# The rows of maxima are sent from SyncE's queue, with another pace for the key and value work

## The chip, the cores and the metric

The kernel runs on one core of one Trainium2 chip. The core has five engines that run at the same time, each through its own list of instructions in order: TensorE (PE, with its weight loads shown apart as PEld), VectorE (DVE), ScalarE (ACT), GpSimd (POOL) and SyncE (SP). SP does no arithmetic here: it issues transfers (DMAs). An instruction that needs another engine's result, or a transfer's, waits for a semaphore, and everything behind it on its engine waits too. The metric is the time of one execution on the device in microseconds (us), lower is better.

## The reference, cut to what matters

Two attention blocks over the same 2048 tokens of width 1024, each with 32 heads of width 32, mixed by a gate per token. Block A is linear attention, block B softmax attention:

```
qkv = x @ wqkv                       # both blocks, own weights
A:  kv  = einsum("bhsd,bhse->bhde", phi(k), v);  z = sum over s of phi(k)
    o   = (phi(q) @ kv) / (phi(q) . z + 1e-6)
B:  p   = softmax(q @ k.T * 32**-0.5);  o = p @ v
g   = sigmoid((x * gate_w).sum(-1))
out = g * (oA @ A_wo) + (1 - g) * (oB @ B_wo)
```

All of it is in float32. The kernel splits an operand into a high and a low part of a narrower type and makes three products of them (L158 to L160: high with high, high with low, low with high).

## The kernel before

**Stages.** First come the projections of block B (L437 to L439 and L475 to L477, up to about 490 us), whose queries and keys go to DRAM (`qk`) and come back head by head. Then the 32 heads of block B run, one after the other. Beside them, in the gaps of PE, runs the linear work of block A ("linear matmuls" below: L993, L158, L159, L160): first the keys and values (`kv`), then the queries (`q`), then the output product (`o`). The end is the output product of block B with the gate.

**A head of block B.** The scores are made twice. `maxima()` makes them with queries in the partitions (L1214), and DVE reduces each 128x512 tile to its row maximum (L1224): 64 tiles a head. `heads_()` makes them again with keys in the partitions (L1403), 64 tiles; ACT takes the exponential of each (L1407), four products a tile of keys give the weighted values (L1508), GpSimd adds the exponentials up (L1452, L1456), with a share done by DVE (L1468). The stream of maxima is 12 or more tiles ahead: while head h is in its second scores, the maxima of head h + 1 are made.

**The rows of maxima.** A maximum is subtracted inside the second scores' matmul: the operand `q` of head h (a tile `big`, three of them in turn) has 96 rows of queries, and rows 96 and 97 hold the negative maxima, as a high and a low part. `rows()` puts them there. DVE reduces the four partial maxima (L1229); PE transposes them (L1235) into a bank; ACT writes the high part `mh` (L1237); DVE makes the low part `ml` (L1240); then two transfers of 8 KB write the two rows (L1246). `mh` and `ml` are two parts of one tile, `m_both`. The first L1403 of the head waits for both transfers.

**What sets the order.** The order on each engine is made when the program is built, by a planner that runs the streams (`maxima`, `heads_`, `linear`, `output`) against clocks of its own (`T`, one for each engine, `use()` adds a cost). A stream yields the time at which it could go on; the planner takes one that can go on now and lags most. Work for DVE is put into a list (`defer`) and taken when DVE is free by the clocks; `tasks` are small jobs that run when their time has come on PE's clock. `rows_ready[h]` is the time at which the planner thinks that the rows have landed: the first second-score of head h isn't taken before it. In the kernel before, the sending is such a task, `send`, which adds 1.1 to ACT's clock.

**The pace of the linear work.** `goal` grows with each tile of second scores by `rates[...]`: 1.4 linear matmuls a tile for `kv` (RATE_KV), 2.6 for `q`, and for `o` what is left (L1674).

**Other lines that are named below.** L833 copies one key/value output out of its bank, and L663 to L665 and L841 follow it; L946 writes a partial sum back into a bank. In the query work DVE divides (L1136, L1137) after ACT has added 1e-6 to the denominators (L1128), PE transposes the result (L797), ACT and DVE split it (L799, L802), and it goes to DRAM as `oA` (L804). L1517 copies the finished values of a head out of their bank. L754 and L759 fold the keys and values into the output weight. L1304 to L1313 turn the sums of a head, L1319 (GpSimd) scales the head's values and L1321 (SP) stores them. L1171 and L1173 load the queries of a later head, L1185 its keys, L658 the operands of `q` and `o` units (two transfers of 512 KB a unit), L1150 stores a result of `o`, and L737 loads output weights.

Of the kernel before, what the change touches and what calls it, by code (L numbers as in the profile page):

```python
# [18 lines left out]
P = 128  # L19
DH = 32  # L20
# [8 lines left out]
WO_SLOT = 4  # L29
RESERVE = 56.0  # L30
RATE_Q = 2.6
RATE_KV = 1.4
AHEAD = {"head": 0, "max": 6, "lin": 40, "kvout": 0, "out": 0}
MM = 0.2275
AV, AV_SWITCH = 0.865, 0.35
# [13 lines left out]
def kernel(  # L49
# [19 lines left out]
    nc = tc.nc  # L69
# [12 lines left out]
    def f32(ap):  # L82
        return ap.bitcast(F32)
# [42 lines left out]
    mh, ml = m_both[:NT], m_both[DH:]  # L126
# [41 lines left out]
    def use(eng, cost, *after):  # L168

        if eng == "dve":  # L170
            after_own[0], own_now[0] = own_now[0], False
        T[eng] = max(T[eng], *after, 0.0) + cost
        return T[eng] + LATENCY[eng]
# [9 lines left out]
    def defer(fn, at, cost=0.6, rank=1, prev=None):  # L183
        item = Later(fn, at, cost, rank, prev)
        later.append(item)
        return item
# [42 lines left out]
    def bank_at(seed=False):  # L229

        times = [ended(readers[b], free[b]) for b in RING if not held[b] and (whole[b] or not seed)]
        return min((at for at in times if at is not None), default=None)

    def take(seed=False, part=False, kept=False):

        idle = [b for b in RING if not held[b] and (whole[b] or not seed)]
        times = {b: ended(readers[b], free[b]) for b in idle}
        b = min(idle, key=lambda b: (times[b] is None, times[b] or 0.0))
        need(readers[b])
        free[b] = ended(readers[b], free[b])  # L240
        readers[b].clear()
        held[b] = True
        whole[b] = whole[b] if kept else not part
        return b

    def give(b, at=0.0, items=()):

        held[b] = False
        free[b] = max(free[b], at)
        readers[b].extend(items)  # L250

    def both(*times):

        return None if None in times else max(times)
# [207 lines left out]
    for np_, js in enumerate(PAIRS):  # L462
# [3 lines left out]
        for pos, k in enumerate(KORDER):  # L466
            while v_at[0] == pos:
                v_next(next(steps))
            i, half = divmod(pos, 2)
# [690 lines left out]
    rows_ready = [None] * H  # L1160
    s_done, st_done = [0], [0]
    tasks = []
# [64 lines left out]
    def rows(h, q, m):  # L1227
        end = use("dve", 0.14)
        nc.vector.tensor_reduce(m, mx[h % 2], AX.X, ALU.max, negate=True)  # L1229

        def turn():
            b = take(part=True)
            pm = bank[b]
            end = use("pe", 0.12, free[b])
            nc.tensor.transpose(pm[:NT, :P], m, ident)  # L1235
            end = use("act", 0.2, end)
            nc.scalar.copy(mh, pm[:NT, :P])  # L1237

            def low(end):
                nc.vector.tensor_sub(ml, pm[:NT, :P], f32(mh))  # L1240

                def send():
                    rows_ready[h] = use("act", 1.1, end) + 2.5
                    for i, part in enumerate((mh, ml)):
                        r = 3 * DH + i
                        nc.scalar.dma_start(f32(q[r:r + 1, :]).rearrange("o (t c) -> o t c", c=P), f32(part))  # L1246

                tasks.append((lambda: end + 0.2, send))

            give(b, 0.0, [defer(low, end, 0.2, 0)])  # L1250

        tasks.append((lambda: both(bank_at(), end), turn))
# [419 lines left out]
    rates = {"q": RATE_Q, "v": 0.0}  # L1672
    rates["kv"] = RATE_KV
    rates["o"] = (cost["o"] - RESERVE) / (steps - cost["q"] / RATE_Q - cost["kv"] / RATE_KV)  # L1674
    goal = [warm]
# [110 lines left out]
```

## Time and profile before

| | us |
|---|---|
| median of 3 runs | 2856.14 (2854.89 to 2862.61) |
| profiled execution, its own time | 2858.8 |
| profiled execution, span | 2857.0 |

| engine | busy us | share of the span |
|---|---|---|
| PE (matmul) | 2820.2 | 99% |
| DVE | 2277.9 | 80% |
| POOL | 1962.8 | 69% |
| ACT | 1691.0 | 59% |

The transfers have a share of 53.6% on SP's queue (q1 in the profile, 394608 packets) and 0.1% on ACT's (q10, 2048 packets: the rows of maxima alone). The granted clock of PE is 0.996 over the run.

A row of the timeline has the start and length in us, the engine, the line, what is done, the tile written and those read; in brackets the idle time ahead of it on its engine and who ended it. A row of the waits has who waited, for whom, the total in us, how many times and the longest. A row of the stretches has the length and for each engine the busy time with the number of instructions, then PE's clock, the DMA share and GB/s. "SPq" and "ACTq" are instructions that issue transfers.

### The profile page before, as it was taken

To read this page: it belongs to the slowest core of one execution; us is meant where nothing else is said; L and a number is where in the kernel's file an instruction comes from. 1 tells how busy PE (TensorE), PEld (TensorE's weight loads), DVE (VectorE), ACT (ScalarE), POOL (GpSimd) and SP (SyncE) were. 2 spreads that over 40 slices of the span, in tenths; PEclk is the share of its full clock that TensorE was granted. 3 is DMA by queue.
4 is the path that set the end of the run, shared out by engine and by line. 5 is a ranking of instruction groups with operands and counts; after the bars stand their busy time and mean duration, and the time that the engine had idled before them with its cause. 6 is when DMAs were issued, how large, how long until landed. Compare 5 with 4: busy or idle time off the path is not lost. (4 is left out here: it accounts for less than half of the span.)

```text
span 2857.0 us, 45633 instructions
## 1 busy us (share of the span) xinstructions
PE 2820.2 (99%) x15552; PEld 2004.8 (70%) x15552; DVE 2277.9 (80%) x3972; ACT 1691.0 (59%) x3206; POOL 1962.8 (69%) x733
## 2 busy tenths in 40 slices
PE   9999999999999999999999999999999999999999
PEld 8888887766666666667666676676666666666687
DVE  7667646888888888888887787788999999997743
ACT  5334320766777677766777566666666666666421
POOL 1212222689999999998989677777889898986000
PEclk9999999999999999999999999999999999999999
DMA  6987888555565433554533456446543434423663
GB/s 194 293 263 230 279 260 274 149 156 155 175 181 162 134 112 105 177 147 132 158 109 114 147 179 205 144 142 180 160 131 111 119 108 143 107 94 122 216 213 103
DMA packets 396890, 470.14 MB, mean 165 GB/s; under 512 B 109366, under 2 KB 240950, under 8 KB 393526
## 3 DMA queue, kind: packets, MB, share of 16 engines
q1 hardware_dynamic: 394608, 466.69, 53.6%
q8 instruction: 123, 2.02, 0.3%
q14 instruction: 111, 0.91, 0.1%
q10 hardware_dynamic: 2048, 0.53, 0.1%
HBM read 318.77 MB, written 146.79 MB: 163 GB/s over the span
## 5 line engine op out<-in xcount | busy, mean ns | idle before, releaser
L1456 POOL TENSOR_TENSOR big<-big,big 128x1536 f32<-128x1536 f32 (+1 forms) x434 | 1557.8, 3589 | 134.7 <-ACT big L1407 113.5
L1224 DVE TENSOR_REDUCE mx<-bank 128x1 f32<-128x512 f32 x2048 | 1344.9, 687 | 246.9 <-PE bank L1214 237.0
L1407 ACT ACTIVATE big<-bank 128x512 f32<-128x512 f32 x2048 | 1163.0, 604 | 437.6 <-PE bank L1403 363.5
L1403 PE MATMUL bank<-big,big 128*128 128x512 f32 x2048 | 807.2, 400 | 6.6 <-ACT big L1407 4.5
L1214 PE MATMUL bank<-big,big 128*128 128x512 f32 x2048 | 802.9, 394 | 9.6 <-DVE mx L1224 6.1
L1403 PEld LDWEIGHTS bank<-big,big 128*128 128x128 f32 x2048 | 382.5, 188 | 171.9 <-issue 44.2
L1214 PEld LDWEIGHTS bank<-big,big 128*128 128x128 f32 x2048 | 385.5, 188 | 107.9 <-DVE mx L1224 19.9
L1508 PE MATMUL bank<-big,mid 128*32 128x512 f32 x4096 | 459.9, 594 | 0.0
L993 PE MATMUL bank<-big,big 128*128 128x512 f32 x1344 | 452.4, 391 | 0.1
L158 PE MATMUL bank<-big,big 128*128 128x512 f32 x896 | 353.1, 394 | 5.7 <-ACT big L270 3.6
L160 PE MATMUL bank<-big,big 128*128 128x512 f32 x896 | 352.1, 393 | 0.5 <-DMA big<-xs 0.5
L1468 DVE TENSOR_TENSOR bank<-bank,big 128x256 f32<-128x256 f32 (+1 forms) x697 | 326.8, 469 | 32.1 <-ACT big L1407 1.0
L159 PE MATMUL bank<-big,big 128*128 128x512 f32 x896 | 351.9, 393 | 0.0
L1508 PEld LDWEIGHTS bank<-big,mid 128*32 128x32 f32 x4096 | 131.8, 110 | 271.6 <-issue 271.3
L993 PEld LDWEIGHTS bank<-big,big 128*128 128x128 f32 x1344 | 251.0, 188 | 54.2 <-ACT bank L946 1.4
L271 DVE TENSOR_TENSOR big<-mid,big 128x512 fp32r<-128x512 f32 x216 | 153.3, 732 | 82.5 <-ACT big L270 82.4
L1452 POOL TENSOR_TENSOR big<-big,big 128x1536 f32<-128x1536 f32 (+1 forms) x31 | 111.6, 3599 | 146.4 <-ACT big L1407 146.4
L416 POOL TENSOR_TENSOR mid<-mid,mid 128x512 f32<-128x512 f32 x16 | 20.7, 1292 | 278.2 <-DVE big L271 251.7
L158 PEld LDWEIGHTS bank<-big,big 128*128 128x128 f32 x896 | 169.5, 189 | 44.9 <-ACT big L270 4.0
L160 PEld LDWEIGHTS bank<-big,big 128*128 128x128 f32 x896 | 169.4, 189 | 36.2 <-DMA big<-xs 1.9
L159 PEld LDWEIGHTS bank<-big,big 128*128 128x128 f32 x896 | 169.7, 189 | 35.6 <-issue 0.8
L270 ACT CAST big<-mid 128x512 fp32r<-128x512 f32 x216 | 130.3, 624 | 94.2 <-POOL mid L417 54.5
(112 smaller groups left out, 2451.4 us busy)
## 6 DMA issues: line engine op xcount, KB each, us to landing
big<-xs SPq DMA_DIRECT2D x80, 512.0 KB
qk<-mid SPq DMA_DIRECT2D x128, 256.0 KB
big<-xt SPq DMA_DIRECT2D x128, 256.0 KB
big<-oA SPq DMA_DIRECT2D x64, 512.0 KB
big<-qk SPq DMA_DIRECT2D x96, 256.0 KB
big<-qk SPq DMA_DIRECT2D x384, 64.0 KB
big<-xs SPq DMA_DIRECT2D x96, 256.0 KB
mid<-in_b_wqkv SPq DMA_DIRECT2D x88, 256.0 KB
```

What stands on the lines that cost most here:

```text
L158: yield nc.tensor.matmul(ps, sh, mh_, start=(kt == 0), stop=False)
L159: yield nc.tensor.matmul(ps, sh, ml_, start=False, stop=False)
L160: yield nc.tensor.matmul(ps, sl, mh_, start=False, stop=(kt == NK - 1))
L271: eng.tensor_sub(lo, src, f32(hi))
L993: nc.tensor.matmul(bank[b], x_, w, start=(k == 0 and j == 0 and not seeded), stop=(k == HK - 1 and j == 2), skip_group_check=seeded)
L1214: nc.tensor.matmul(bank[b], q[:, t * P:(t + 1) * P], k[:, j * C:(j + 1) * C], start=True, stop=True)
L1224: nc.vector.tensor_reduce(m[:, t, j:j + 1], bank[b], AX.X, ALU.max)
L1403: nc.tensor.matmul(bank[b], k[:, t * P:(t + 1) * P], q[:, j * C:(j + 1) * C], start=True, stop=True)
L1407: nc.scalar.activation(pr_t[i][:, j * C:(j + 1) * C], bank[b], AF.Exp, scale=SCALE)
L1456: nc.gpsimd.tensor_add(lacc[:, :qp], lacc[:, :qp], pr(t)[:, :qp])
L1468: nc.vector.tensor_add(lacc[:, qp:][:, sl] if t == NT - 1 else l_b[:, sl], l_b[:, sl], src[:, sl])
L1508: nc.tensor.matmul(av_b[j * DH:(j + 1) * DH, :], v[:, t, :], pr(t)[:, j * C:(j + 1) * C], start=(t == 0), stop=(t == NT - 1))
```

## The change

The two transfers of a head go out from SP's queue, right behind the low part in the order in which the program is written, and no longer as a task of their own from ACT's queue. The planner's ACT clock isn't charged for them any more, and it takes the rows as landed 2.5 us after the low part. RATE_KV goes from 1.4 to 1.45. Lines behind the change move up by 4: L1403 is L1399 after, L1517 is L1513, L1321 is L1317, and the transfers are L1244.

```
-RATE_KV = 1.4
+RATE_KV = 1.45
...
             def low(end):
+                rows_ready[h] = end + 2.5
                 nc.vector.tensor_sub(ml, pm[:NT, :P], f32(mh))
-
-                def send():
-                    rows_ready[h] = use("act", 1.1, end) + 2.5
-                    for i, part in enumerate((mh, ml)):
-                        r = 3 * DH + i
-                        nc.scalar.dma_start(f32(q[r:r + 1, :]).rearrange("o (t c) -> o t c", c=P), f32(part))
-
-                tasks.append((lambda: end + 0.2, send))
+                for i, part in enumerate((mh, ml)):
+                    r = 3 * DH + i
+                    nc.sync.dma_start(f32(q[r:r + 1, :]).rearrange("o (t c) -> o t c", c=P), f32(part))
```

Since the planner's clocks run otherwise, the order of all engines differs from the first heads on. Three places follow.

ACT at the rows of head 28 (`big_3937` to `big_3939` hold exponentials, `bank_...` scores), before:

```order
L1407 ACTIVATE big_3938<-bank_302 128x512
L1237 CAST m_both<-bank_296 16x128
L1407 ACTIVATE big_3938<-bank_298 128x512
L1407 ACTIVATE big_3938<-bank_302 128x512
L1407 ACTIVATE big_3938<-bank_298 128x512
L1246 DMA big_262<-m_both 1x16x128 x2
L1407 ACTIVATE big_3939<-bank_302 128x512
```

and after:

```order
L1403 ACTIVATE big_3938<-bank_302 128x512
L1237 CAST m_both<-bank_297 16x128
L1403 ACTIVATE big_3938<-bank_301 128x512
L1403 ACTIVATE big_3938<-bank_302 128x512
L1403 ACTIVATE big_3938<-bank_301 128x512
L1403 ACTIVATE big_3939<-bank_302 128x512
```

The two sends are gone from between the exponentials; the rest reads alike but for the banks.

SP at the same head, from the store of the values of an earlier head (`oB`) on; `l_sb` are the turned sums, `big_264` takes operands of the output product, `big_263` keys of head 29, before:

```order
L1313 DMA l_sb<-r_186 128x1x512
L1321 DMA oB<-mid_292 32x4x128 x4
L1185 DMA big_263<-qk_0_7_151 32x512
L1185 DMA big_263<-qk_1_7_159 32x512
L1185 DMA big_263<-qk_0_7_151 32x512
L658 DMA big_264<-oA_4_99 128x1024
L658 DMA big_264<-oA_4_115 128x1024
L1150 DMA ra_172<-mid_295 128x512
```

and after:

```order
L1309 DMA l_sb<-r_186 128x1x512
L1317 DMA oB<-mid_292 32x4x128 x4
L658 DMA big_264<-oA_4_99 128x1024
L658 DMA big_264<-oA_4_115 128x1024
L1150 DMA ra_172<-mid_295 128x512
L1185 DMA big_263<-qk_0_7_151 32x512
L1185 DMA big_263<-qk_1_7_159 32x512
L1185 DMA big_263<-qk_0_7_151 32x512
L1244 DMA big_262<-m_both 1x16x128 x2
L1185 DMA big_263<-qk_0_7_151 32x512
```

The rows now stand in SP's line, here behind a store that waits for GpSimd, two operands of 512 KB and three pieces of keys; the unit of the output product has come ahead of the keys.

ACT at the first query unit (`dn` are its denominators), before:

```order
L1407 ACTIVATE big_3937<-bank_302 128x512
L1407 ACTIVATE big_3938<-bank_297 128x512
L1517 COPY mid_292<-bank_300 128x512
L1128 ACTIVATE dn_258<-dn_258,eps 128x16
L799 CAST mid_289<-bank_302 128x512
```

and after:

```order
L1403 ACTIVATE big_3935<-bank_301 128x512
L1403 ACTIVATE big_3935<-bank_298 128x512
L1403 ACTIVATE big_3936<-bank_301 128x512
L1128 ACTIVATE dn_258<-dn_258,eps 128x16
L1403 ACTIVATE big_3936<-bank_301 128x512
```

The small instruction on the denominators stood behind the copy of a finished head and now stands between exponentials.

## The prediction

> **What bounds the kernel now.** I read the page's head and its chain of waits first.
>
> ```profile
> span 2857.0 us, 45633 instructions
> PE 2820.2 (99%) x15552; PEld 2004.8 (70%) x15552; DVE 2277.9 (80%) x3972; ACT 1691.0 (59%) x3206; POOL 1962.8 (69%) x733
> PE 39%; DVE 2%; DMA 1%; ACT 0%; issue 0%; SPq 0%; ACTq 0%
> ```
>
> TensorE (PE) is the bound, and the row transfers' old engine (ACT) is at 59% and has 0% of the chain. Then the timeline, to see how far "busy" can be trusted:
>
> ```profile
> 1509.61 0.39 PE L1403 MATMUL bank<-big,big 128*128 128x512 f32 x1
> 1509.84 0.39 PE L1214 MATMUL bank<-big,big 128*128 128x512 f32 x1
> 1510.07 0.39 PE L993 MATMUL bank<-big,big 128*128 128x512 f32 x1
> ```
>
> A matmul is recorded for 0.39 us, but the next starts 0.23 us later: 0.227 us is its real price, and a stop of under 0.16 us doesn't show as idle. Recorded idle is a lower bound. Where it lies, by stage (projections; heads beside key/value work; heads beside query work; heads beside the output product; the end):
>
> ```profile
> 0.00:490.00 490.00, 485.66 (x2120) 400.47 (x2121) 314.29 (x473) 175.95 (x309) 116.44 (x93) 1.00 0.82 255
> 490.00:1550.00 1060.00, 1051.40 (x6566) 715.26 (x6568) 912.08 (x1629) 750.61 (x1518) 957.02 (x381) 1.00 0.50 148
> 1550.00:2010.00 460.00, 445.49 (x2389) 311.04 (x2382) 369.36 (x649) 284.00 (x532) 342.38 (x97) 0.99 0.53 164
> 2010.00:2655.00 645.00, 643.15 (x3616) 422.05 (x3615) 585.61 (x1005) 429.51 (x771) 546.94 (x164) 1.00 0.41 121
> 2655.00:2857.00 202.00, 194.51 (x871) 156.02 (x869) 96.60 (x219) 50.93 (x78) 0.00 (x0) 0.99 0.53 173
> ```
>
> After the stretch's length the columns are PE, weight loads, DVE, ACT, POOL. PE idles 4.3, 8.6, 14.5, 1.9 and 7.5 us, 37 of 2857. The two orders hold the same number of matmuls of every line, so the change can only remove or add waits of PE; and the first and the last stage stand in the same order. (ACT's order has no send left and SP's has all 64, so the change does what it says.) The second and third stage are where it can gain.
>
> **Part 1, the key/value pace (RATE_KV).** Stretches from one head's row transposition (L1235) to the next one's, heads counted from 0: heads 8 and 12, then 5, 6, 7, 13, 14, 15.
>
> ```profile
> 1032.00:1092.70 60.70, 60.68 (x365) 40.20 (x364) 53.13 (x96) 41.32 (x82) 58.13 (x20) 1.00 0.34 97
> 1288.30:1353.90 65.60, 65.60 (x419) 45.58 (x418) 57.72 (x105) 45.49 (x91) 56.41 (x21) 1.00 0.41 120
> 821.80:893.60 71.80, 71.21 (x454) 49.35 (x453) 60.28 (x110) 54.76 (x116) 68.57 (x32) 1.00 0.59 176
> 893.60:962.60 69.00, 67.63 (x477) 44.77 (x476) 60.55 (x114) 48.58 (x106) 66.62 (x31) 1.00 0.52 151
> 962.60:1032.00 69.40, 68.10 (x464) 44.63 (x463) 57.98 (x107) 51.19 (x110) 66.66 (x32) 1.00 0.50 151
> 1353.90:1423.70 69.80, 68.94 (x441) 46.33 (x440) 59.83 (x108) 52.48 (x111) 66.56 (x30) 1.00 0.52 158
> 1423.70:1491.50 67.80, 66.27 (x473) 44.28 (x472) 59.96 (x112) 48.29 (x104) 57.66 (x23) 1.00 0.39 114
> 1491.50:1560.40 68.90, 66.49 (x449) 41.46 (x449) 57.89 (x108) 50.21 (x109) 62.16 (x31) 1.00 0.43 129
> ```
>
> In the order head 8 has 67 linear matmuls and head 12 has 90: 23 more in 4.9 us, 0.21 each, as it should be without stops. From head 8 at 0.227 each, heads 5, 6, 7, 13, 14, 15 with 106, 80, 82, 93, 78, 69 linear matmuls should take 69.5, 63.6, 64.1, 66.6, 63.2, 61.2 us; they lose 2.3, 5.4, 5.3, 3.2, 4.6, 7.7, together **28 us**. These are the heads in which 6 or 7 key/value outputs (L833) come, against 1 to 4 elsewhere, and where DVE and ACT are fullest. The fewer linear matmuls there are to an output, the more is lost: 2.3 and 3.2 us at 15 to an output, 5.4, 4.6 and 7.7 at 11 or 12 (mean 5.9).
>
> The higher rate puts more linear matmuls into a head. After, the six heads have 91, 81, 91, 84, 82, 123 of them, with 6, 7, 6, 7, 7, 3 outputs: 15, 12, 15, 12, 12 and 41 to an output. By the same reading they lose 2.7, 5.9, 2.7, 5.9, 5.9 and nearly nothing (0.7 as head 8): 24. I take **-5 us**; bounds -12 (a third of what is left goes too) and +3 (clumps as tight as before, at other places).
>
> The linear matmuls come out of the last stage's heads, which then hold 60 to 62 instead of 63 to 65. Head 28 there:
>
> ```profile
> 2424.00:2483.60 59.60, 59.60 (x330) 39.81 (x329) 56.00 (x97) 39.52 (x71) 56.65 (x18) 1.00 0.38 99
> ```
>
> PE's share falls by 2.5 x 0.227 = 0.6 us to 59.0, still above POOL's 56.65 and DVE's 56.0. **+0.5 us**; 0 to +6 if each of ten heads gives its 0.6 back.
>
> **Part 2, ACT is rid of the sends.**
>
> ```profile
> L1246 ACTq DMA_DIRECT2D big<-m_both x64: 510/544/1380, 492.0 to 2604.9; - x64
> PE bank L1403 <- ACT big L1407: 4.5, 5, 2.7
> PE bank L1214 <- ACT big L1407: 2.4, 4, 0.9
> ```
>
> 64 x 0.544 = 35 us of issuing leave ACT, 1.1 us a head. ACT isn't the bound, so this is worth only what PE waits for late exponentials: 4.5 + 2.4 = 6.9 us recorded in all. **-3 us**, nearly half of it; bounds 0 and -6.9.
>
> **Part 3, the query stage.** The epsilon of a denominator (L1128, ACT) holds up a division on DVE and four transpositions on PE. In ACT's order before it stands three times right behind the copy of a finished head (L1517), and once behind the mix casts (L759). The first of these:
>
> ```profile
> 1579.23 0.59 ACT L1517 COPY mid<-bank 128x512 f32<-128x512 f32 x1 [5.36 <-PE bank L1508]
> 1580.05 0.25 DVE L1136 RECIPROCAL dn<-dn 128x16 f32<-128x16 f32 x1 [4.20 <-ACT dn L1128]
> 1581.08 0.66 PE L797 MATMUL bank<-ident,mid 128*128 128x128 f32 x4 [1.95 <-DVE mid L1137]
> 1586.81 0.50 PE L1214 MATMUL bank<-big,big 128*128 128x512 f32 x1 [2.54 <-DVE mx L1224]
> ```
>
> PE stops for 1.95 us, and 2.54 more when DVE's backlog reaches it. The new order has L1128 behind that copy once and behind the casts once: two places fewer, 2 x 1.95 = **-4 us**; bounds -9 (the after-effect too) and +6 (as many new places of another kind, such as the weight loads).
>
> **Part 4, the rows on SyncE's queue (SP).** Before, in head 28 (transposition, cast, low half, the two sends, first score), and what SP issued just ahead:
>
> ```profile
> 2422.21 1.80 SPq L1321 DMA_DIRECT2D oB<-mid  x4
> 2424.05 0.27 PE L1235 MATMUL bank<-ident,mneg 128*16 128x128 f32 x1
> 2424.11 1.33 SPq L1185 DMA_DIRECT2D big<-qk  x3
> 2425.78 0.28 DVE L1240 TENSOR_TENSOR m_both<-bank,m_both 16x128 fp32r<-16x128 f32 x1
> 2426.03 1.17 ACTq L1246 DMA_DIRECT2D big<-m_both  x2
> 2431.99 0.40 PE L1403 MATMUL bank<-big,big 128*128 128x512 f32 x1
> q10 hardware_dynamic: 32, 0.01, 4.5%
> ```
>
> The last row is ACT's queue between 2427.8 and 2428.6; after 2428.5 nothing of it is left, so a send lands about 1.9 us after its issue at best. The worst is in head 24, right behind two loads of 512 KB and four of 256 KB:
>
> ```profile
> 2181.59 1.14 SPq L658 DMA_DIRECT2D big<-oA  x2
> 2183.64 2.40 SPq L737 DMA_DIRECT2D big<-in_a_wo  x4
> 2184.79 5.82 DMA big<-m_both
> 2190.75 0.47 PE L1403 MATMUL bank<-big,big 128*128 128x512 f32 x1 [0.78 <-DMA big<-m_both]
> ```
>
> After, the budget from transposition to first score is 32 to 34 matmuls in heads 21 to 30, 7.5 us (7.9 before), and 20 in head 31 (28 before), 4.8 us. The low half ends 2.0 us after the transposition; SP's second issue starts then or 0.6 later, so the row lands at 4.4 with the best landing and at 8.4 with the worst. It is late only in the second case. In the new SP order 1 MB of oA loads stands just ahead in heads 22, 24, 26, 28, 30. I take +1.5 us for these and head 31, less the wait of head 24 (0.78), whose a_wo loads now come behind the rows: **+0.5 us**; bounds -0.8 and +11 (six heads at 1.8 us).
>
> What the other side of SP's queue pays: loads behind a row wait for DVE's low half too, at most the 1.7 us between transposition and low half; they are prefetches of a later head or unit, so nothing.
>
> A rule speaks against this part. The Trainium skill, "DMA: Bandwidth & Descriptors", section "Queues, rings and completion order", says that SP and ACT each own a row of rings and that a DMA engine changes between rows packet by packet, so on ACT's own ring rows pass the loads, and on SP's they stand in line. The trace agrees only in part: the 5.82 us in head 24 were on ACT's own ring. By the rule the rows land later by what stands ahead of them, and the sum is that of the late rows below; by head 24's row it was no shelter before, and the sum stands.
>
> **Sum.** -5 + 0.5 - 3 - 4 + 0.5 = **-11 us**, against the profiled execution's 2858.8 us (span and 1.8 around it). That one lies 2.7 above the median of 2856.14, inside the runs' 2854.89 to 2862.61; the median minus 11 is **2845 us**.
>
> **Rivals.** *The waits only move*: the planner makes a new order, and clumps and misplaced epsilons turn up elsewhere, as the bounds +3 and +6 allow. For it: most of the loss sits at a few places that no term of the planner aims at. Half of ACT's 3 us is left: 2854. *The rows come late*: in line behind the loads on SP's ring, PE stops at each late head's first score. It decides at a landing of 7.5 - 2.2 = 5.3 us. At 7 us eleven late heads wait 1.7 us each and the dozen earlier heads with 35 to 40 matmuls of budget (7.9 to 9.1 us) about 0.6 each: +26, less 11 of gains: 2871. For it: head 24's 5.82, and no late head has more than 34 matmuls of budget (7.7 us). Against it: most landings are short, as in head 28. That is the case on the slower side.
>
> **Numbers.** Forecast 0.55 (its own range 2836 to 2851), waits that move 0.32 (2848 to 2862), late rows 0.13 (2862 to 2880). A measurement of this kernel can tell about 0.3%, 8.6 us, from no change. Faster by more: four fifths of the first case and a tenth of the second, 0.47; slower: 0.12; within: 0.41. The range 2834 to 2861 leaves out most of the late rows and little else.
>
> **What would show it.** Right: heads 5 to 7 and 13 to 15 lose under 25 us by the same count; idle of the third stage falls from 14.5 to about 10; no first score waits over 1.5 us for m_both. Wrong: a wait of L1399 on m_both in many heads, or DVE waits of L1214 in the last stage.

## The result, and the profile after

The changed kernel takes 2885.11 us (median of 4 runs, 2880.69 to 2888.69) against 2859.38 (2854.89 to 2863.00) for the kernel before on the same chip: a ratio of 1.0090, 95% interval 1.0067 to 1.0113. It is **slower by 0.9%, 26 us**, where 11 us less was forecast; the time lies 24 us above the upper end of the range. The profiled execution is the highest of the four, 2888.69 us.

The head of the page and its chain of waits, after:

```profile
span 2886.8 us, 45829 instructions
PE 2826.8 (98%) x15552; PEld 2007.9 (70%) x15552; DVE 2277.9 (79%) x3980; ACT 1695.1 (59%) x3206; POOL 1965.0 (68%) x733
PE 38%; DVE 2%; DMA 1%; ACT 0%; issue 0%; SPq 0%; DVEq 0%; ACTq 0%
```

The matmuls are the same 15552, every engine's busy time is within 7 us of before, and the span is 30 us longer: most of that is waits. The stages, cut at the same events as before (the borders are 1.3 us ahead of the first row transposition, 6 us behind the last L993, 2 us behind the last L797, and 52 to 53 us behind the last row transposition):

```profile
0.00:493.00 493.00, 485.47 (x2120) 400.32 (x2121) 313.94 (x473) 175.85 (x309) 116.45 (x93) 1.00 0.82 254
493.00:1540.00 1047.00, 1027.36 (x6402) 699.57 (x6404) 888.27 (x1587) 734.33 (x1476) 926.35 (x372) 1.00 0.50 148
1540.00:2005.00 465.00, 445.73 (x2395) 310.39 (x2391) 370.39 (x649) 284.03 (x534) 333.71 (x96) 0.98 0.53 164
2005.00:2684.00 679.00, 672.41 (x3778) 440.87 (x3771) 608.91 (x1056) 449.46 (x809) 588.45 (x174) 0.99 0.39 117
2684.00:2886.00 202.00, 195.79 (x868) 156.77 (x867) 96.41 (x218) 51.41 (x78) 0.00 (x0) 0.98 0.53 173
```

PE idles 7.5, 19.6, 19.3, 6.6 and 6.2 us, 59 in all against 37: 22 more. The rest of the 30 is in stops too short to show and in matmuls at a lower clock (last section). The loss sits in few places. Heads 9, 12, 16 and 22 after (transposition to transposition):

```profile
1103.00:1182.70 79.70, 73.25 (x452) 50.13 (x451) 58.19 (x105) 52.70 (x107) 66.53 (x30) 0.96 0.48 143
1310.60:1383.30 72.70, 69.42 (x429) 47.83 (x427) 59.01 (x108) 48.69 (x98) 61.13 (x25) 0.98 0.52 154
1601.30:1710.10 108.80, 93.94 (x524) 63.38 (x523) 78.81 (x137) 57.68 (x111) 54.77 (x16) 0.94 0.50 161
2092.20:2158.60 66.40, 60.69 (x327) 39.66 (x326) 55.60 (x97) 39.19 (x71) 54.16 (x17) 0.95 0.35 107
```

and heads 9, 16 and 22 before (head 12 stands in the prediction, with no idle time):

```profile
1092.70:1157.90 65.20, 65.20 (x401) 44.57 (x400) 56.88 (x102) 45.99 (x94) 58.50 (x23) 1.00 0.43 129
1560.40:1655.80 95.40, 89.24 (x482) 62.61 (x481) 72.80 (x129) 54.28 (x101) 66.91 (x19) 0.96 0.45 138
2060.80:2122.40 61.60, 61.40 (x363) 39.75 (x361) 58.41 (x101) 42.21 (x75) 56.39 (x18) 1.00 0.45 136
```

The lengths can't be compared, since the orders put other numbers of matmuls into a head; the idle time can: 6.5, 3.3, 14.9 and 5.7 us against 0, 0, 6.2 and 0.2. These four heads hold 24 us of new idle time, more than the net 22. Who waits there, in the timeline of head 9:

```profile
1153.87 1.28 POOL L1315 TENSOR_TENSOR mid<-mid,l_sb 128x512 f32<-128x512 f32 x1
1155.18 1.79 SPq L1317 DMA_DIRECT2D oB<-mid  x4
1157.01 1.41 SPq L586 DMA_DIRECT2D big<-wt  x3
1159.92 0.62 ACT L638 CAST big<-big 128x512 fp32r<-128x512 f32 x1 [5.51 <-DMA big<-wt]
1161.09 0.79 PE L1399 MATMUL bank<-big,big 128*128 128x512 f32 x1 [5.28 <-ACT big L1403]
```

Read upwards: PE waits for an exponential, ACT stands at a cast of a weight operand (`wt`), whose load was issued only at 1157.01, because SP stood at the store of a head's values (L1317) until GpSimd had scaled them (L1315). SP's own waits from 1149 to 1160 us say it:

```profile
SPq L1317 <- POOL mid L1315: 4.7, 1, 4.7
```

In head 16:

```profile
1653.55 2.83 SPq L762 DMA_DIRECT2D wa<-mid  x1
1656.43 8.51 SPq L737 DMA_DIRECT2D big<-in_a_wo  x4
1664.98 0.90 SPq L804 DMA_DIRECT2D oA<-mid  x2
1670.56 0.58 ACT L799 CAST mid<-bank 128x512 fp32r<-128x512 f32 x1 [15.03 <-DMA oA<-mid]
1672.52 1.06 PE L1282 MATMUL bank<-big,ones 128*32 128x512 f32 x1 [10.35 <-DVE big L1464]
```

ACT can't overwrite a query result (L799) before its predecessor has been stored (L804); that store is behind four loads of output weights (L737), and these behind the stores of the fold (L762: keys and values folded into the weights, L754 to L762). And in head 22 the row of maxima itself is late:

```profile
2091.63 0.52 SPq L762 DMA_DIRECT2D wa<-mid  x1
2092.23 0.27 PE L1235 MATMUL bank<-ident,mneg 128*16 128x128 f32 x1
2092.58 1.68 SPq L658 DMA_DIRECT2D big<-oA  x2
2096.12 0.32 SPq L1150 DMA_DIRECT2D ra<-mid  x1
2098.69 1.23 SPq L1244 DMA_DIRECT2D big<-m_both  x2
2105.78 0.77 PE L1399 MATMUL bank<-big,big 128*128 128x512 f32 x1 [5.71 <-DMA big<-m_both]
```

6.5 us pass from the transposition to the issue, and 6.8 from there to the landing of the first row (2105.46 by the trace's semaphore events; the second row 2105.64).

### The profile page after: what moved, and what is told of

Its sections match the earlier page's. It is cut to its first block, busy times and chain, and to the rows that moved or that the text cites. A ratio compares the mean times of both kernels' runs of the same rounds, so it can differ in the third digit from the quotient of the medians.

```text
span 2886.8 us, 45829 instructions
## 1 busy us (share of the span) xinstructions
PE 2826.8 (98%) x15552; PEld 2007.9 (70%) x15552; DVE 2277.9 (79%) x3980; ACT 1695.1 (59%) x3206; POOL 1965.0 (68%) x733
## 5 line engine op out<-in xcount | busy, mean ns | idle before, releaser
L1403 ACT ACTIVATE big<-bank 128x512 f32<-128x512 f32 x2048 | 1166.3, 603 | 432.4 <-PE bank L1399 373.0
L1399 PE MATMUL bank<-big,big 128*128 128x512 f32 x2048 | 809.1, 401 | 17.7 <-ACT big L1403 9.7
L1399 PEld LDWEIGHTS bank<-big,big 128*128 128x128 f32 x2048 | 383.6, 188 | 180.6 <-issue 52.2
L993 PE MATMUL bank<-big,big 128*128 128x512 f32 x1344 | 453.8, 393 | 0.3 <-ACT bank L946 0.3
L993 PEld LDWEIGHTS bank<-big,big 128*128 128x128 f32 x1344 | 252.7, 189 | 56.6 <-ACT bank L946 3.5
```

The lines of the kernel that those rows point to most:

```text
L993: nc.tensor.matmul(bank[b], x_, w, start=(k == 0 and j == 0 and not seeded), stop=(k == HK - 1 and j == 2), skip_group_check=seeded)
L1399: nc.tensor.matmul(bank[b], k[:, t * P:(t + 1) * P], q[:, j * C:(j + 1) * C], start=True, stop=True)
L1403: nc.scalar.activation(pr_t[i][:, j * C:(j + 1) * C], bank[b], AF.Exp, scale=SCALE)
```

## Experiments: the queue or the order

All ratios are to the kernel before, run beside them on the same chip; 0.1% is 2.9 us. Two theories: the rows lose time because they stand in SP's line (**queue**), or the order that the planner makes with the new pace and clocks does (**order**). Four kernels separate queue and pace. The planner's clocks have no kernel of their own; they alone differ between k1 and k4 and between k3 and k2.

A stop that is named from here on is counted from start to start of the matmuls, which is about 0.16 us more than the idle time in the rows.

**k1**, the kernel before with the queue alone:

```
-                        nc.scalar.dma_start(f32(q[r:r + 1, :])...
+                        nc.sync.dma_start(f32(q[r:r + 1, :])...
```

> The kernel before, with only the queue of the rows' transfers changed from ACT's to SP's; the planner still charges its ACT clock, so PE, DVE and POOL keep the order of before. Queue theory (the rows lose time because they stand in SP's line, and hold up what stands behind them there): most of the 26 us is lost here too, 2870 to 2885 us, with waits of the first second score on the rows or of casts on loads behind the rows. Order theory (the planner's new order loses them): 2854 to 2860 us, and the stops of PE at the heads 9, 12, 16 and 17 of the changed kernel aren't there.

**k2**, the changed kernel with the rows on ACT again:

```
-                    nc.sync.dma_start(f32(q[r:r + 1, :])...
+                    nc.scalar.dma_start(f32(q[r:r + 1, :])...
```

> The changed kernel with the rows sent from ACT's queue again, at the place in the program where it sends them from SP; PE, DVE and POOL keep the order of the changed kernel. Queue theory: 2855 to 2862 us. Order theory: 2874 to 2884 us; the stops of 10.5 us in head 16, about 7 in head 9 and 3.4 in head 12 stay, and only the 6 us at the first second score of head 22 go, less what the sends cost ACT.

**k3**, the kernel before with the pace alone:

```
-RATE_KV = 1.4
+RATE_KV = 1.45
```

> The kernel before with only RATE_KV 1.45. If the pace makes the loss: 2870 to 2885 us. If the planner's clocks (ACT no longer charged, rows taken as landed earlier) or the queue make it: 2850 to 2860 us; by the prediction's first part alone 2850 to 2855.

**k4**, the changed kernel without the pace:

```
-RATE_KV = 1.45
+RATE_KV = 1.4
```

> The changed kernel with RATE_KV back at 1.4: the queue and the planner's clocks alone. If the pace makes the loss: 2853 to 2862 us. If the queue or the clocks make it: 2870 to 2885 us. If every order that the planner makes has a few waits of its own at places of chance, this one has neither head 16's 10.5 us nor head 9's 7, but others, and lies between 2855 and 2880.

| kernel | pace | rows on | planner's clocks | us | ratio, 95% interval |
|---|---|---|---|---|---|
| before | 1.4 | ACT | before | 2859.11 | 1 |
| k1 | 1.4 | SP | before | 2873.80 | 1.0057 (1.0042 to 1.0071) |
| k4 | 1.4 | SP | after | 2863.93 | 1.0022 (1.0013 to 1.0030) |
| k3 | 1.45 | ACT | before | 2888.88 | 1.0110 (1.0094 to 1.0126) |
| after | 1.45 | SP | after | 2885.11 | 1.0090 (1.0067 to 1.0113) |
| k2 | 1.45 | ACT | after | 2894.86 | 1.0134 (1.0115 to 1.0153) |

**The pace makes the loss**: 1.1% alone (k3), and 0.0090 - 0.0022 = 0.7% on top of the queue. The queue with its clocks costs 0.2% at 1.4, and at 1.45 nothing (0.9% against 1.1%). k3 lies above its expected range by 4 us. With the rows on ACT it shows the very stops of the changed kernel: heads 9, 12 and 16 (10.3 us there), and even the one at the rows of head 22:

```profile
2092.20 0.27 PE L1235 MATMUL bank<-ident,mneg 128*16 128x128 f32 x1
2098.17 3.26 ACTq L1246 DMA_DIRECT2D big<-m_both  x2
2101.54 2.08 ACT L1407 ACTIVATE big<-bank 128x512 f32<-128x512 f32 x4 [6.60 <-DMA big<-m_both]
```

That one isn't the queue's doing: the send waits on either engine, and on ACT the exponentials wait with it. k1 lies in the range of the queue theory. k4 lies between its first two ranges and inside the wide third one, that of waits at places of chance. The queue costs something, less than the pace. What it costs is at other heads, 25 and 27 above all; of k4's waits for rows

```profile
PE bank L1399 <- DMA big<-m_both: 11.0, 3, 5.7
```

4.3 and 5.7 us are at their first scores; the first row landed 9.85 and 7.95 us after its issue. The third, 1.1 us, is at head 24. k2 came out above both of its expectations. Its profiled execution (span 2884.9) is below all its other runs, so the 10 us by which the rows on ACT are worse there can't be placed.

**k8**, the kernel before with RATE_KV 1.42, asks whether a higher pace costs steadily:

> The kernel before with RATE_KV 1.42. If a higher pace costs steadily: a third to a half of the 30 us that 1.45 cost, 2868 to 2875. If the cost is where single transfers fall in SP's line: anything between 2852 and 2890, with stops at other heads than at 1.45, each behind a wait of SP.

2878.16 us, 1.0072 (1.0057 to 1.0087), above the range of a steady price and inside the wide other one. Stops of 2.5 to 4.7 us stand at heads 5, 9, 17, 19 and 25; head 12's is gone, and PE idles 1.8 us in head 16 where it idles 14.5 at 1.45 (k3). The largest waits of ACT for transfers are now those of k8's profile:

```profile
ACT mid L799 <- DMA oA<-mid: 21.1, 5, 5.8
ACT big L1407 <- DMA big<-m_both: 13.5, 4, 5.0
```

The places speak for single collisions, and the time alone would not. Two paces are too few to say how others scatter.

## Experiments: which waits in SP's line

Now SP's order alone is changed, in the changed kernel; every other engine keeps its instructions in their order. **k5** moves the loads of output weights, **k6** the store of the values, **k7** both:

```
-        for i in range(HK):
-            nc.sync.dma_start(mix_hi[i], a_wo[...])
+        tasks.append((lambda at=T["pe"] + 10.0: at, lambda: [
+            nc.sync.dma_start(mix_hi[i], a_wo[...]) for i in range(HK)]))
```

```
-                for j in range(NJ):
-                    nc.sync.dma_start(oB_d[...], avs[...])
+                put = (lambda at=T["pe"] + 8.0: at, lambda: [
+                    nc.sync.dma_start(oB_d[...], avs[...]) for j in range(NJ)])
+                f_task.append(put); tasks.append(put)
```

> The changed kernel with the four loads of output weights (L737) issued 10 us later by the planner's clock; every other engine keeps its order, on SP only these four move, in four places. If the stop of 10.5 us in head 16 comes from stores of the query results (L804) that stand on SP behind these loads, which wait for the fold's stores: the wait of ACT L799 on oA falls from 15 to under 5 us, and the time is 2885 less 8 to 12, 2873 to 2878. If that stop has another cause: 2883 to 2888 with the same stop.

> The changed kernel with the store of a head's values (L1317) put on SP 8 us later by the planner's clock; nothing else moves. If the stops in heads 9 (6.8 us) and 12 (3.4 us) come from the operands out of wt (L586) that stand on SP behind that store while it waits for GpSimd: both stops go, and the time is 2870 to 2877. If they come from something else (the transfers themselves are slow, or ACT is late): 2883 to 2888.

> Both moves together in the changed kernel. If the loss of the higher pace is these waits in SP's line: 2860 to 2867 us, what is left being head 22's 6 us and the queue. If the pace costs by itself (more matmuls between the heads, clumps): 2875 to 2888.

k6 is in its range (2872.89 us, 1.0049, 1.0030 to 1.0069): head 9's stop is gone (1.3 us left), so it was the store that waits for GpSimd. Head 12's 3.4 stayed at 3.0, so that one was not. **k5 missed**: 2882.10 us, 1.0088 (1.0073 to 1.0104), between its two ranges; the wait of L799 went from 15.0 to 11.7 only. k7 is a little above its range (2868.39 us, 1.0039, 1.0026 to 1.0052). Why k5 missed shows when the landings are set beside the issues. From the semaphore events of the trace, the changed kernel in head 16:

```
                  issued              landed
L762 wa store     1650.84 - 1651.37   1659.57
L762 wa store     1651.42 - 1651.93   1662.06
L762 wa store     1653.00 - 1653.51   1664.59
L762 wa store     1653.55 - 1656.38   1667.17
L737 weights, 1st 1656.43 - 1658.76   1667.81
L737 weights, 4th 1664.61 - 1664.93   1669.81
L804 oA store     1664.98 - 1665.41   1670.46
```

Everything lands in the order of issue; the fourth load of weights is issued as the third store lands. Each store of the fold lands 2.5 to 2.6 us after the one before it; the loads of the same 256 KB are 0.5 to 0.9 apart. Moving L737 out of the way lets L804 be issued earlier, but it still lands behind the stores (in k7 issued from 1644.28 on, landed at 1656.08). So the stores themselves are slow. Two stretches of the changed kernel, between the landing ahead of the first store listed and its own, and during the loads of weights (DMA share and GB/s are the last two columns):

```profile
1656.75:1659.55 2.80, 2.80 (x16) 2.32 (x15) 2.48 (x5) 0.00 (x0) 2.30 (x1) 1.00 0.29 107
1667.85:1670.00 2.15, 0.00 (x0) 0.00 (x0) 0.00 (x0) 0.00 (x0) 0.00 (x0) 0.50 1.00 349
```

A share of 0.29 of 16 engines is 4.6 of them, at a third of the rate. The semaphore that tells of a landing is updated 5 times for each of the 32 stores of the fold, and 16 times for each load of weights. The store's target in DRAM is a pattern of 4 blocks x 32 rows x 512. By the Trainium skill, "DMA: Bandwidth & Descriptors", section "Rules for kernel authors", an outermost dimension of a size c below 16 confines a transfer to at most c engines; the 0.29 agrees with c = 4.

**k10** writes each of these stores as four transfers of 32 rows, in the changed kernel; **k11** is k7 with the same edit, **k12** the kernel before with it, **k13** is k4 with it:

```
-                nc.sync.dma_start(wa_d[p][a][c][:, r * DH:(r + 1) * DH, :], f32(src))
+                for i in range(HK): nc.sync.dma_start(wa_d[p][a][c][i, r * DH:(r + 1) * DH, :], f32(src[i * DH:(i + 1) * DH, :]))
```

> The changed kernel with each store of the fold (L762, 256 KB, which holds the line of transfers for about 2.6 us in the records) written as four transfers of 32 rows, 64 KB each (such pieces of the keys follow one another at 0.19 us). Same order on every engine. If the clumps of these stores in the line are what makes head 16's 10.5 us and head 22's 5.9 us: both stops fall to under 3 us and the time to 2868 to 2876. If the number of transfers ahead counts and not their time: 2885 to 2900, as SP issues 96 more.

> The changed kernel with all three edits of SP's line: the values' stores and the weights' loads later, and the fold's stores in four pieces. If the pace itself costs nothing and gains what the prediction's first part said: 2845 to 2852. If it neither costs nor gains once SP's line is clear: 2852 to 2858. If it costs by itself: over 2862.

> The kernel before with the fold's stores in four pieces. At its own pace the stores fall where little waits for them; its stops in heads 16 and 18 (11.9 and 11.3 us with everything) are mostly the epsilon's. Expected 2850 to 2857; much below 2850 would mean that the same clumps cost the kernel before as well.

> The changed kernel with RATE_KV 1.4 and the fold's stores in four pieces. The first score of head 25 waits 4.4 us there for rows behind such a store, that of head 27 5.8 us behind loads of wa and oA: the first should go and the second stay, 2864 less 4 to 6, 2857 to 2861.

| kernel | us | ratio, 95% interval | L799 on oA | L638 on wt | L1399 on m_both |
|---|---|---|---|---|---|
| after | 2885.11 | 1.0090 (1.0067 to 1.0113) | 15.0 | 10.5 | 6.2 |
| k5 | 2882.10 | 1.0088 (1.0073 to 1.0104) | 11.7 | 12.6 | 6.2 |
| k6 | 2872.89 | 1.0049 (1.0030 to 1.0069) | 17.1 | 4.9 | 3.6 |
| k7 | 2868.39 | 1.0039 (1.0026 to 1.0052) | 11.8 | 6.4 | 3.3 |
| k10 | 2872.27 | 1.0052 (1.0037 to 1.0067) | 11.5 | 10.7 | 0.7 |
| k11 | 2858.90 | 1.0000 (0.9991 to 1.0009) | 6.1 | 5.6 | - |

(The last three columns are totals of the waits in each profile, in us.) **With all three edits the changed kernel is as fast as the kernel before as it stands.** Of its 0.90%, moving the store that waits for GpSimd takes away 0.41% (k6), and splitting the fold's stores 0.38% (k10). The split gives the kernel before 0.21% as well (k12), so the fair comparison is with the kernel before under the same edits, in the next section. The pieces land 0.2 to 0.5 us after one another in head 16, and their semaphores are updated 16 times each. k10 came out at 2872.27, inside its range; head 22's wait is gone, but head 16's stop fell to 7.1 us only, not under 3. There SP now spends 0.45 us on each of 16 pieces before it issues L804 at 1653.03, and the loads of weights still stand between; only with these moved too (k11) the wait falls to 6.1. k11 came out a little above its middle range. k12 is 2851.33 us, 0.9979 (0.9969 to 0.9988): **faster than both kernels**, with one line of the kernel before changed. k13 is 2856.23, 0.9995 (0.9984 to 1.0005), 0.8 us below its range, and the waits went as expected: head 25's is gone, head 27's stayed (4.3 us).

## Experiments: what is left with SP's line clear

Four kernels with all three edits: **k14** on the kernel before, **k15** on k4, **k16** on k2, **k17** on k1.

> The kernel before with the three edits of SP's line (the values' stores 8 us later, the weights' loads 10 us later, the fold's stores in four pieces). Beside the one of them that gave 7 us (the fold's stores), the other two have little to move here: 2846 to 2853.

> The changed kernel with RATE_KV 1.4 and the three edits. Against the kernel before with the same edits this shows the queue with the planner's new clocks: 2850 to 2857, with the 4 us wait of head 27 for its rows behind loads of wa and oA left. If ACT's freed time were worth the 3 us that the prediction gave it: below the kernel before with the same edits.

> The changed kernel's order at 1.45 with the rows sent from ACT and the three edits; its fellow with the rows on SP took 2859. If a send that has to wait on ACT stops the exponentials: 2860 to 2870. If with SP's line clear the queue makes no difference: 2855 to 2861.

> The order of the kernel before with the rows on SP and the three edits: the queue alone, with nothing of the planner changed. The 15 us that the queue cost in this order were waits of the heads 25 and 27 for their rows; head 25's goes with the fold's stores in pieces, head 27's stays: 2853 to 2862.

| kernel, three edits | pace | rows on | planner's clocks | us | ratio, 95% interval |
|---|---|---|---|---|---|
| k14 | 1.4 | ACT | before | 2852.06 | 0.9974 (0.9964 to 0.9985) |
| k17 | 1.4 | SP | before | 2857.66 | 0.9996 (0.9984 to 1.0008) |
| k15 | 1.4 | SP | after | 2853.16 | 0.9976 (0.9965 to 0.9988) |
| k11 | 1.45 | SP | after | 2858.90 | 1.0000 (0.9991 to 1.0009) |
| k16 | 1.45 | ACT | after | 2865.83 | 1.0017 (1.0008 to 1.0027) |

All four lie in a range that was expected. Of the changed kernel's 26 us, 7 are left when both kernels have the three edits (k14 to k11). The pace's part is down from 19 us to 0.0024 x 2858 = 7 (k15 to k11), the queue's with its clocks from 6 to nothing (k14 to k15). The queue alone costs 6 us in the order of before (k14 to k17), and k17's profile has 5.8 of them at one place:

```profile
PE bank L1403 <- DMA big<-m_both: 5.8, 1, 5.8
```

It is the first score of head 27, whose row landed 8.65 us after its issue, behind loads of `wa` and 1 MB of `oA`. At 1.45 the rows on SP are 5 us better than on ACT (k16 to k11); what causes these 5 us stays open.

The 7 us left of the pace: k11 still stops 3.2 us in head 12, at a `wt` load that lands 6 us after its issue, right behind L1309. That load spreads the inverse sums of a head over 32 partitions for each of four blocks, so its source too has 4 outermost, and its semaphore too is updated 5 times. It landed 4.7 us or more after its issue all 31 times in the kernel before (5.7 in the mean). **k18** (on k11) and **k19** (on k14) make four loads of it:

```
-                nc.sync.dma_start(l_sb, r_d[h % 2].unsqueeze(1).to_broadcast([NJ, DH, C]))
+                for j in range(NJ): nc.sync.dma_start(l_sb[j * DH:(j + 1) * DH, :], r_d[h % 2][j:j + 1, :].to_broadcast([DH, C]))
```

> The changed kernel with the three edits and the load that spreads a head's inverse sums (L1309, 31 times, 256 KB) made as four loads of 32 partitions. If the rest of the pace's cost is loads that land behind such transfers: head 12's 3.2 us go, and the time is that of the kernel before with the same four edits, 2846 to 2854. If the pace costs by itself: 2855 to 2860, 5 to 8 above its fellow.

> The kernel before with the same four edits. It has no stop at such a load, so little changes from 2852: 2847 to 2854. Above 2856 would mean that the 93 more issues on SP cost more than the shorter loads give.

| kernel, four edits | pace | rows on | us | ratio, 95% interval |
|---|---|---|---|---|
| k18 | 1.45 | SP | 2850.61 | 0.9974 (0.9965 to 0.9984) |
| k19 | 1.4 | ACT | 2848.20 | 0.9969 (0.9957 to 0.9981) |

The pieces land 2.0 us after their issue in the mean, head 12's stop is 1.3 us, and the rest of the cost is gone: the changed kernel with four edits (pace, queue and clocks together) stands 0.05% above the kernel before with the same four, inside both intervals. **k19 has the lowest time of this study**, 0.3% below the kernel before.

## Why the prediction was wrong

**The pace (forecast -4.5, measured +31 alone, +19 beside the queue).** The step that failed is "they lose 2.7, 5.9, 2.7, 5.9, 5.9 and nearly nothing (0.7 as head 8): 24", and with it the bounds -12 and +3. The six heads after:

```profile
830.60:900.90 70.30, 69.86 (x454) 46.55 (x453) 60.80 (x112) 52.30 (x110) 68.83 (x31) 1.00 0.56 168
900.90:969.10 68.20, 67.00 (x459) 43.92 (x458) 58.45 (x109) 48.96 (x106) 62.91 (x29) 1.00 0.50 147
969.10:1039.50 70.40, 69.08 (x473) 47.03 (x473) 58.48 (x109) 52.77 (x111) 67.53 (x33) 1.00 0.54 153
1383.30:1452.70 69.40, 67.72 (x448) 44.63 (x447) 60.03 (x111) 51.70 (x111) 63.16 (x28) 1.00 0.40 119
1452.70:1522.00 69.30, 67.79 (x462) 44.35 (x461) 59.88 (x111) 50.77 (x108) 59.41 (x25) 1.00 0.41 120
1522.00:1601.30 79.30, 78.09 (x485) 52.61 (x483) 65.50 (x119) 52.86 (x106) 67.28 (x29) 1.00 0.44 137
```

With 91, 81, 91, 84, 82 and 123 linear matmuls, from head 8 of before as in the prediction, they lose 4.1, 4.3, 4.3, 4.8, 5.2 and 5.9 us: 29, not 24. The head with 41 linear matmuls to an output, forecast at nearly nothing, has the most; 96 of its 123 are matmuls of the query work. The number of linear matmuls to an output, on which the term rested, was not a guide; the reading had also left out head 7 of before, which lost 5.3 with 14 to an output. What does decide these losses is not shown. About 4 us of either sum are no loss at all, but the small key/value matmuls (L689), 80 to 128 of them in these heads against 32 in head 8, at 0.010 us each.

But this is 5 us of the miss. The rest was not in the term at all: it asked only how the pace crowds PE, DVE and ACT. The pace also sets where each transfer of the linear work comes in SP's line, and there it met the value stores and the fold's stores. Where the prediction looked at the loads in that line (part 4), it put them at nothing, as "prefetches of a later head or unit"; in head 9 ACT stood 5.5 us for one of them.

**ACT's freed time (forecast -3) and the rows on SP (+0.5, bounds -0.8 and +11).** The runs measure the two together: +16 us in the order of before, +6 with the planner's new clocks, and with the line cleared by three edits +6, nothing, and -5 at 1.45. The sum of -2.5 that the prediction gave the two together lies among these by luck. The step that failed is "the row lands at 4.4 with the best landing and at 8.4 with the worst". The worst landing of before, 5.82 us, was behind 2 MB of loads, and I took loads for the worst that can be ahead. A store of the fold holds the line for 2.5 us at 256 KB. Rows took 9.85 and 7.95 us in k4, and in the changed kernel's head 22 the issue alone came 6.5 us after the transposition. The point from which the rival of late rows decides, a landing of 5.3 us, was about right: a row that landed 5.5 us after its issue cost 1.1 us in k4, and one at 4.7 us cost 0.7 in k1. But long waits were met at one or two heads, not at eleven, and they were 4 to 6 us, not 1.7.

**The query stage (forecast -4).** The total of PE's waits at L797 for DVE's division, before and after:

```profile
PE bank L797 <- DVE mid L1137: 6.7, 4, 2.0
```

```profile
PE bank L797 <- DVE mid L1137: 7.9, 3, 4.3
```

One stop fewer instead of two, and a longer one: +1.2, inside the bounds. The step "two places fewer, 2 x 1.95" took each place for a stop of its own; the long one, in head 17, is gone in k6, so it hung on SP's line too. The third stage's idle time went from 14.5 to 19.3 instead of about 10; 10.4 of the 19.3 are the one stop in head 16.

**The rivals.** "The waits only move" had the right mechanism and a bound far too small: +3 and +6 for new places, where four heads took 24. Its own reason, that the loss sits at places that no term of the planner aims at, was the better guide than my sum. "The rows come late", the slower rival, has one head with a long wait in the changed kernel (head 22, 5.7 us), and k3 loses 5.1 us there with the rows on ACT.

**The rule on rings.** The prediction set aside, on one row of head 24, the rule of the Trainium skill, "DMA: Bandwidth & Descriptors", section "Queues, rings and completion order", by which a DMA engine changes packet by packet between the two rings, so that a transfer on ACT's own ring can pass loads on SP's. Head 22 shows both sides: on ACT (k3) the row was issued at 2098.17 and landed at 2103.12, ahead of a load that SP had issued at 2094.31 (landed at 2105.82); on SP (after) it was issued at 2098.69 and landed at 2105.46, behind that load (2104.61). The trace agrees with the rule there. It was no gain, since what held the rows was their issue: the second row, which the score needs too, was issued on ACT at 2100.92 and landed at 2105.63, and on SP it landed at 2105.64.

## What to carry to other kernels

Where one engine issues nearly all transfers, its line is a resource like an engine: a change that shifts the pace of a stream moves its loads and stores past the others, so look up, for each line that can wait there, what may stand behind it. Ask of each transfer how long it holds the line, from landing to landing, and not only its size. If a change of a planner's constant loses time at a few places, clear these places before judging the constant: with four edits in both kernels, the change with its 1.45 costs nothing that can be measured, where the pace had cost 19 to 31 us. And one line on the slow store is worth 6 us to the kernel before.

## What was not expected of the hardware

**Eight transfers in flight, whoever issues them.** The transfers of SP and ACT share eight semaphores in turn (289 or 290 transfers on each in the changed kernel), and an issue waits until the transfer eight back has landed. Whether the chip could hold more in flight is not shown. In head 22 the row was issued at 2098.69, when the fold's store that used the same semaphore had landed at 2098.62; in k3 ACT's send started at 2098.17, after such a store's landing at 2098.10. So slow stores issued by SP stopped ACT.

**A stop costs more than itself.** PE's granted clock behind head 9's stop (the third column from the end; the stop lasts from 1155.8 to 1161.1):

```profile
1157.00:1159.00 2.00, 0.00 (x0) 0.00 (x0) 0.00 (x0) 0.00 (x0) 1.54 (x1) 1.00 0.61 155
1161.00:1163.00 2.00, 1.91 (x5) 1.52 (x6) 0.65 (x2) 2.00 (x6) 2.00 (x3) 0.50 0.94 273
1165.00:1167.00 2.00, 2.00 (x9) 1.62 (x6) 1.14 (x3) 1.78 (x5) 2.00 (x1) 0.50 0.87 282
1167.00:1169.00 2.00, 2.00 (x10) 1.60 (x9) 1.52 (x3) 1.09 (x2) 2.00 (x3) 0.93 0.06 23
```

It is 0.50 until about 6 us after the restart, and the matmuls there follow one another at 0.43 us and not at 0.23. Against head 8 of before at 0.227 a linear matmul, head 9 loses 10.1 us, of which 6.8 are its two stops. PE counts as busy in the slow stretch, so the idle time of a stage is a lower bound for this reason too. Over the whole run the granted clock is 0.992, and 0.996 before.
